# Moving tiles within SBUF: first weights 128 bytes past a multiple of 256, gate tiles 192 past, with no instruction changed

## The chip, the cores and the metric

The kernel runs on one core of one Trainium2 chip. The metric is the device time of one execution in microseconds (us), the median of three runs. TensorE (PE in the profile) multiplies matrices: it loads a stationary operand of 128 x 128 (PEld, LDWEIGHTS) and streams a moving operand past it (PE, MATMUL). Both are read from SBUF; the sums go to PSUM. DVE is VectorE, ACT ScalarE, POOL GpSimd, SP the engine that issues most transfers.

## The reference

Windowed attention with four sink positions over 4 batches, 8 heads, 768 positions and 64 channels, and after it a feed-forward layer over its 3072 rows. Cut to what matters:

```python
scores = scale * np.matmul(q, k.transpose(0, 1, 3, 2))
keep = is_sink | in_window            # n_sink 4, window 128
a = softmax(np.where(keep, scores, -1e9))
x = (a @ v).transpose(0, 2, 1, 3).reshape(3072, 512)
h = x @ w_in                          # 512 x 2048
g = h - np.tanh(h)
out = g @ w_out                       # 2048 x 512
```

Everything is float32.

## The kernel before

The 3072 rows are cut into 12 chunks of 256. Attention for a chunk leaves x transposed in SBUF. The feed-forward layer goes through 8 groups of 256 hidden channels, so there are 12 x 8 = 96 steps of chunk and group, and each step has two halves.

The first half (`mm1`, L700) makes h, 256 hidden channels by 256 rows, as 24 matmuls with a first-weight tile `w0` as the stationary operand (128 x 128) and the chunk's x as the moving one (128 x 256). Float32 accuracy is had from two rounded parts of every operand: `xh` and `xl` are x's high and low part, and a `w0` tile holds a high and a low part too. Each pair of 128 x 128 of weights goes high by `xh`, high by `xl`, low by `xh`.

The gate (`gate`, L705 to L716) is ACT's tanh, DVE's subtraction, ACT's rounding to `gh` and DVE's remainder `gl`. The second half (`mm2`, L748) adds to out 12 matmuls with a slice of `gh` or `gl` as the stationary operand (128 x 128) and a row of the second weights `w1` as the moving one (128 x 512). Step n's second half stands behind step n + 1's first half on TensorE, so the gate has time.

Attention of later chunks is woven between steps: scores `s` (L496, stationary `q`, moving `ks`, 128 x 260), transposes `t` (L575, stationary the probabilities `p`, moving the identity), and x (L629, stationary `v`, moving `pt`). The first 12 units of scores take raw float32 operands that lie for that time in the places of weight tiles (L489, `qk`).

A recording layer (`Work`) notes each piece of work with its engine, an estimated duration and a due time, and sets each engine's order before anything runs. It doesn't know addresses.

Tiles lie in SBUF in the order in which their pools are opened: every pool takes the next free bytes of each partition. Slices of `w0`, `w1`, x, `gh` and `gl` that a matmul reads start at multiples of 512 bytes from the start of their tile, so a tile's place modulo 256 is that of all its operands. The scores are the exception: slices of `ks` start 0, 16, 32 or 48 bytes past a multiple of 256, by head and by half of the chunk. `GAP` is 16, the width in float32 of a tile that nothing reads or writes; it only takes 64 bytes.

Of the kernel before, what the change touches and what calls it, by code (L numbers as in the profile page):

```python
# [9 lines left out]
F32 = mybir.dt.float32  # L10
# [8 lines left out]
P = 128  # L19
# [19 lines left out]
GAP = 16  # L39
# [3 lines left out]
def kernel(  # L43
# [50 lines left out]
    with tc.If(bad == 0) as cmp:  # L94
        _banded(tc, qd, kp, vp, vs, masks, w_in, w_out, ident, pts, early, out)
# [146 lines left out]
def _banded(tc, qd, kp, vp, vs, masks, w_in, w_out, ident, pts, early, out):  # L242
    nc = tc.nc
    et = mybir.EngineType
    with ExitStack() as ctx:

        def pool(name, bufs, **kw):
            return ctx.enter_context(tc.tile_pool(name=name, bufs=bufs, **kw))

        pool("gap", 1).tile([P, GAP], F32, tag="gap", name="gap")  # L250
        w0pool, wmpool, kpool = pool("w0pool", 1), pool("wmpool", 2), pool("kpool", 2)
        w1pool, cpool = pool("w1pool", 1), pool("cpool", 1)
        wpools = w0pool, w1pool
        qpool, vpool, hpool = pool("qpool", 2), pool("vpool", 3), pool("hpool", 1)
        xpool, gpool = pool("xpool", 2), pool("gpool", 2)
        spool, pp, sm = pool("spool", 1), pool("pp", 2), pool("sm", 4)
        ps_s, ps_t, ps_x = pool("ps_s", 1, space=PSUM), pool("ps_t", 1, space=PSUM), pool("ps_x", 1, space=PSUM)
        ps_h, ps_o = pool("ps_h", 2, space=PSUM), pool("ps_o", 1, space=PSUM)
        work = Work()
# [794 lines left out]
```

## Time and profile before

| | before |
|---|---|
| time, median of 3 runs | 686.6 us (686.59 to 687.09) |
| the profiled execution: its time | 687.03 us |
| the profiled execution: span from first to last instruction | 685.2 us |
| TensorE busy, matmuls | 671.9 us, 98% of the span |
| TensorE busy, weight loads | 598.4 us, 87% |
| VectorE busy | 426.9 us, 62% |
| ScalarE busy | 366.8 us, 54% |
| TensorE's granted clock, mean | 0.998 of full speed |

A matmul's recorded duration runs from its first read to its last result, and the next one starts long before that end. So the time that a matmul takes from the engine is the distance between starts, or between ends, and not the duration; trains of equal matmuls in the chain of work or in the timeline show it.

### The profile page before, as it was taken

How to read it: one execution, taken by the hardware profiler on the slowest of the kernel's cores; microseconds unless marked ns; L12 is line 12 of the kernel's file. 1: busy time of each engine (PE TensorE's matmuls, PEld its weight loads, DVE VectorE, ACT ScalarE, POOL GpSimd, SP SyncE). 2: the span in 40 equal slices, each digit the busy share in tenths (PEclk: the TensorE clock that was granted, in tenths of full speed). 3: DMA queues.
4: the chain of work that ended last, by engine and by line, in shares of the span. 5: the costliest groups of instructions: out<-in, count | busy, mean ns of one | idle time of the engine just before them, and what ended most of it. 6: DMA issues, size and time to landing. Idle time of an engine off the chain costs nothing.

```text
span 685.2 us, 12423 instructions
## 1 busy us (share of the span) xinstructions
PE 671.9 (98%) x4604; PEld 598.4 (87%) x4604; DVE 426.9 (62%) x1084; ACT 366.8 (54%) x1001; POOL 52.0 (8%) x201
## 2 busy tenths in 40 slices
PE   7999999999999999999999999999999999999996
PEld 5777899999889989989988998998898898998986
DVE  6889999837845647656655665565554755663221
ACT  5996433347754646456545645555555645644222
POOL 6220010000000010000001000001000000000000
PEclk9999999999999999999999999999999999999999
DMA  6789800012221132012103102122112111100000
GB/s 207 242 251 381 345 1 2 4 64 81 55 81 37 30 106 56 28 34 90 48 28 109 55 28 91 28 54 80 38 34 83 55 28 59 59 1 1 32 1 35
DMA packets 31713, 52.14 MB, mean 76 GB/s; under 512 B 3228, under 2 KB 21020, under 8 KB 31644
## 3 DMA queue, kind: packets, MB, share of 16 engines
q1 hardware_dynamic: 31340, 50.93, 22.9%
q8 instruction: 38, 0.62, 0.4%
q10 hardware_dynamic: 304, 0.33, 0.2%
q14 instruction: 31, 0.25, 0.1%
HBM read 44.96 MB, written 6.29 MB: 75 GB/s over the span
## 4 chain that ended last, share of the span: by engine, by line
PE 87%; ACT 6%; DVE 3%; SPq 1%; issue 1%; DMA 0%; POOL 0%; POOLq 0%; ACTq 0%
PE o L748 38%; PE h L700 36%; PE s L496 5%; PE x L629 5%; PE t L575 2%; ACT p L548 2%; ACT p L522 2%; PE x L623 1%; DVE pt L589 1%; DVE pt L169 1%; DMA qk<-qd 0%; ACT gh L712 0%; ACT ks L453 0%; DVE pt L167 0%; PE x L606 0%
## 5 line engine op out<-in xcount | busy, mean ns | idle before, releaser
L700 PE MATMUL h<-xh,w 128*128 128x256 f32 x1536 | 285.5, 281 | 0.0
L700 PEld LDWEIGHTS h<-xh,w 128*128 128x128 f32 x1536 | 240.7, 188 | 1.7 <-issue 0.2
L700 PE MATMUL h<-xl,w 128*128 128x256 f32 x768 | 215.0, 280 | 0.0
L748 PE MATMUL o<-w,gh 128*128 128x512 f32 x768 | 197.2, 397 | 0.8 <-ACT gh L712 0.5
L748 PEld LDWEIGHTS o<-w,gh 128*128 128x128 f32 x768 | 137.7, 188 | 27.7 <-ACT gh L712 2.1
L700 PEld LDWEIGHTS h<-xl,w 128*128 128x128 f32 x768 | 146.3, 191 | 1.4
L748 PE MATMUL o<-w,gl 128*128 128x512 f32 x384 | 104.9, 394 | 0.0
L705 ACT ACTIVATE graw<-h 128x512 f32<-128x512 f32 x96 | 56.9, 592 | 89.7 <-PE h L700 89.7
L522 ACT ACTIVATE p<-p,st 128x132 f32<-128x132 f32 x192 | 76.1, 399 | 52.3 <-DVE st L514 51.4
L716 DVE TENSOR_TENSOR gl<-h,gh 128x512 fp32r<-128x512 f32 x96 | 66.1, 688 | 48.8 <-ACT gh L712 48.6
L708 DVE TENSOR_TENSOR h<-h,graw 128x512 f32<-128x512 f32 x96 | 66.4, 691 | 44.4 <-ACT graw L705 44.0
L748 PEld LDWEIGHTS o<-w,gl 128*128 128x128 f32 x384 | 70.8, 188 | 15.0 <-issue 1.0
L712 ACT CAST gh<-h 128x512 fp32r<-128x512 f32 x96 | 55.6, 579 | 49.9 <-DVE h L708 49.8
L508 DVE COPY_PREDICATED s<-above,s 128x256 f32<-128x256 uint32 x80 | 34.0, 425 | 72.6 <-PE s L496 72.4
L548 ACT ACTIVATE p<-p,st 128x132 f32<-128x132 f32 x192 | 61.9, 396 | 5.7 <-DVE st L543 5.3
L514 DVE CUSTOM_DVE_ANT_0 p<-s,mask 128x132 f32<-128x132 f32 x192 | 48.9, 292 | 8.6 <-POOL qraw L347 2.7
L553 POOL CAST z<-p 128x16 fp32r<-128x16 f32 x48 | 10.2, 213 | 495.8 <-ACT p L548 493.9
L496 PE MATMUL s<-ks,q 128*128 128x260 f32 x288 | 46.2, 282 | 0.0
L463 ACT CAST q<-qraw 128x512 fp32r<-128x512 f32 x36 | 22.4, 622 | 43.8 <-PE s L496 41.8
L496 PEld LDWEIGHTS s<-ks,q 128*128 128x128 f32 x288 | 42.3, 188 | 4.0 <-issue 0.4
L645 DVE TENSOR_TENSOR xl<-x,xh 128x512 fp32r<-128x512 f32 x24 | 16.5, 688 | 44.3 <-ACT xh L641 44.3
L458 DVE TENSOR_TENSOR ks<-kraw,ks 64x392 fp32r<-64x392 f32 x72 | 40.4, 561 | 2.2
(77 smaller groups left out, 574.2 us busy)
## 6 DMA issues: line engine op xcount, KB each, us to landing
qraw<-qd SPq DMA_DIRECT2D x36, 256.0 KB, 2.7
wraw<-w_in SPq DMA_DIRECT2D x16, 512.0 KB, 8.1
wraw<-w_out SPq DMA_DIRECT2D x16, 512.0 KB, 10.0
kraw<-kp SPq DMA_DIRECT2D x37, 196.0 KB, 2.6
v<-vp SPq DMA_DIRECT2D x27, 256.0 KB, 2.9
out<-ob SPq DMA_DIRECT2D x24, 256.0 KB, 2.2
qk<-kp SPq DMA_DIRECT2D x8, 196.0 KB, 5.0
qk<-qd SPq DMA_DIRECT2D x16, 64.0 KB, 4.7
```

Of the source, the lines that this page charges most:

```text
L458: nc.vector.tensor_tensor(k[o, h, :], t[r, :], k[r, h, :].bitcast(F32), op=ALU.subtract)
L496: nc.tensor.matmul(ps[h][:, :WIN], lhsT=q[:, h, t * P : (t + 1) * P], rhs=rhs, start=i == 0, stop=i == 1,)
L514: nc.vector.tensor_tensor_reduce(out=pr[u][:, j, :], in0=ps[h][:, P:WIN], in1=mask[:, kind, :], scale=-0.125, scalar=BIG, op0=ALU.add, op1 ...
L522: nc.scalar.activation(e, e, AF.Exp, bias=st[u][:, j : j + 1], scale=-1.0, accum_out=st[u][:, 4 + j : 5 + j],)
L548: nc.scalar.activation(pr[u][:, j, :], pr[u][:, j, :], AF.Copy, scale=s[:, 8 + j : 9 + j])
L629: nc.tensor.matmul(xps[key][(p - p0) // 2][h * 64 : h * 64 + 64, p % 2, a:z], lhsT=vt[cc, i][:, hd : hd + D], rhs=rhs, start=False, stop=p ...
L700: nc.tensor.matmul(hps[n][:, f, :], lhsT=w, rhs=x, start=r == 0, stop=r == 11)
L705: nc.scalar.activation(gr[n], hps[n], AF.Tanh)
L708: nc.vector.tensor_tensor(hps[n], hps[n], gr[n], op=ALU.subtract)
L712: nc.scalar.copy(gh[n], hps[n])
L716: nc.vector.tensor_tensor(gl[n], hps[n], gh[n].bitcast(F32), op=ALU.subtract)
L748: nc.tensor.matmul(ops[cc, t], lhsT=(gh, gh, gl)[i][n][:, f, t * P : (t + 1) * P], rhs=wt[1, g][:, (0, 1, 0)[i], f, :], start=first and no ...
```

## The change

The pools are opened in another order, and the filling tile is 128 bytes instead of 64 and stands elsewhere. No instruction is added, removed or moved: on every engine the order of instructions is the same in both programs. Only the places in SBUF differ. In bytes past a multiple of 256:

| tile | read by | before | after |
|---|---|---|---|
| `w0` (first weights), and `qk` lent from them | weight loads of L700 | 64 | 128 |
| `xh`, `xl` | moving operand of L700 | 0 | 0 |
| `gh`, `gl` | weight loads of L748 | 0 | 192 |
| `w1` (second weights) | moving operand of L748 | 0 | 0 |
| `q`, `ks` of later chunks | L496 | 0 | 0 |
| `p` of later chunks (two buffers) | weight loads of L575 | 0, 64 | 128, 192 |
| `p` and `ob` in `wmpool` | L575, stores | 64, 128 | 0, 64 |
| `kraw` (two buffers) | ACT, DVE, first units' L489 | 192, 224 | 0, 32 |
| `graw` | DVE | 0 | 192 |
| `vsink` | weight loads of L623 | 0 | 192 |

Modulo 512 the same holds with `w0` at 320 before and 384 after, and `gh`, `gl` at 0 and 192.

```diff
-        pool("gap", 1).tile([P, GAP], F32, tag="gap", name="gap")
-        w0pool, wmpool, kpool = pool("w0pool", 1), pool("wmpool", 2), pool("kpool", 2)
+        wmpool, w0pool, pp = pool("wmpool", 2), pool("w0pool", 1), pool("pp", 2)
         w1pool, cpool = pool("w1pool", 1), pool("cpool", 1)
         wpools = w0pool, w1pool
         qpool, vpool, hpool = pool("qpool", 2), pool("vpool", 3), pool("hpool", 1)
-        xpool, gpool = pool("xpool", 2), pool("gpool", 2)
-        spool, pp, sm = pool("spool", 1), pool("pp", 2), pool("sm", 4)
+        xpool, kpool = pool("xpool", 2), pool("kpool", 2)
+        pool("gap", 1).tile([P, 2 * GAP], F32, tag="gap", name="gap")
+        gpool, spool, sm = pool("gpool", 2), pool("spool", 1), pool("sm", 4)
```

## Rows read from the trace of the kernel before

**Rows 1.** The page: busy time, share of the span and instructions of each engine, and TensorE's granted clock in 40 slices of the span (9 is 90% or more).

```profile
PE 671.9 (98%) x4604; PEld 598.4 (87%) x4604; DVE 426.9 (62%) x1084; ACT 366.8 (54%) x1001; POOL 52.0 (8%) x201
PEclk9999999999999999999999999999999999999999
```

**Rows 2.** Who waited for whom, TensorE's matmuls: us in total, times, longest.

```profile
PE warm L92 <- POOL pt L105: 3.3, 1, 3.3
PE t L575 <- DVE pt L589: 1.3, 2, 0.9
PE t L575 <- ACT p L548: 0.8, 1, 0.8
...
PE o L748 <- ACT gh L712: 0.5, 2, 0.3
```

**Rows 3.** The page's groups: line, engine, operation, output and operands, shapes, count; busy us, mean ns of one; idle time before.

```profile
L700 PE MATMUL h<-xh,w 128*128 128x256 f32 x1536 | 285.5, 281 | 0.0
L700 PE MATMUL h<-xl,w 128*128 128x256 f32 x768 | 215.0, 280 | 0.0
L748 PE MATMUL o<-w,gh 128*128 128x512 f32 x768 | 197.2, 397 | 0.8 <-ACT gh L712 0.5
L748 PE MATMUL o<-w,gl 128*128 128x512 f32 x384 | 104.9, 394 | 0.0
L496 PE MATMUL s<-ks,q 128*128 128x260 f32 x288 | 46.2, 282 | 0.0
...
L700 PEld LDWEIGHTS h<-xl,w 128*128 128x128 f32 x768 | 146.3, 191 | 1.4
```

**Rows 4.** The chain of work that ended last, its 25 longest pieces in order of time: start us, us, engine, output and line, count of instructions. Of L700 the list has three trains of 48 at 5.45 us, all shown, ten of 48 at 5.65 and five of 42 at 4.95, of which the first and the last stand here.

```profile
273.39 5.47 PE o L748 x24
279.33 5.65 PE h L700 x48
292.57 4.95 PE h L700 x42
308.93 5.45 PE h L700 x48
...
418.24 5.45 PE h L700 x48
...
545.96 5.50 PE o L748 x24
...
581.54 5.45 PE h L700 x48
...
635.33 5.65 PE h L700 x48
...
669.47 4.95 PE h L700 x42
```

**Rows 5.** Groups of matmuls (PE) and of weight loads (PEld) in two stretches inside trains of L700, columns as in rows 3: first 311.5 to 314.2 us, then 323.9 to 326.6 us.

```profile
L700 PE MATMUL h<-xh,w 128*128 128x256 f32 x17 | 3.0, 277 | 0.0
L700 PEld LDWEIGHTS h<-xl,w 128*128 128x128 f32 x8 | 1.5, 188 | 0.0
...
L700 PE MATMUL h<-xh,w 128*128 128x256 f32 x16 | 2.9, 281 | 0.0
L700 PEld LDWEIGHTS h<-xl,w 128*128 128x128 f32 x8 | 1.5, 192 | 0.0
```

**Rows 6.** Two trains of L748 in the timeline, eight matmuls with `gh` and four with `gl` each: start us, us from the first start to the last end, instruction, count. Then their groups, columns as in rows 3, in the stretch of each.

```profile
138.34 2.00 PE L748 MATMUL o<-w,gh 128*128 128x512 f32 x8
140.19 1.07 PE L748 MATMUL o<-w,gl 128*128 128x512 f32 x4
...
548.58 1.98 PE L748 MATMUL o<-w,gh 128*128 128x512 f32 x8
550.39 1.07 PE L748 MATMUL o<-w,gl 128*128 128x512 f32 x4
...
L748 PE MATMUL o<-w,gh 128*128 128x512 f32 x7 | 1.8, 393 | 0.0
...
L748 PE MATMUL o<-w,gh 128*128 128x512 f32 x8 | 2.0, 389 | 0.0
```

**Rows 7.** The chain from 305 to 355 us, short pieces between the trains, columns as in rows 4.

```profile
308.45 0.48 PE s L496 x4
...
314.38 0.44 PE t L575 x4
314.82 2.75 PE o L748 x12
317.57 0.47 PE s L496 x4
...
318.74 2.74 PE o L748 x12
```

**Rows 8.** Engines in three stretches of the steps: us, busy us of each engine and instructions, clock, DMA share, GB/s.

```profile
60.00:158.50 98.50, 98.05 (x638) 88.53 (x637) 83.33 (x107) 40.92 (x68) 2.75 (x3) 1.00 0.29 113
186.00:440.00 254.00, 253.74 (x1812) 228.84 (x1811) 150.43 (x398) 138.08 (x378) 14.31 (x60) 1.00 0.19 57
440.00:684.00 244.00, 239.76 (x1664) 215.64 (x1662) 120.95 (x312) 117.35 (x311) 10.52 (x45) 1.00 0.13 39
```

**Rows 9.** The gate tile `gh`: instructions that write or read it, count, duration in ns (least, median, most), first and last start.

```profile
L712 ACT CAST gh<-h x96: 558/586/598, 55.4 to 675.9; 128x512 fp32r<-128x512 f32 x96
L716 DVE TENSOR_TENSOR gl<-h,gh x96: 676/690/693, 56.9 to 676.5; 128x512 fp32r<-128x512 f32 x96
```

**Rows 10.** The page's groups of small matmuls whose stationary tile moves, and its transfers: tiles, queue, count, KB each, median us from issue to landing.

```profile
L575 PE MATMUL t<-ident,p 128*128 128x128 f32 x192 | 29.4, 275 | 2.5 <-DVE pt L589 1.3 <-ACT p L548 0.8 <-ACT pt L582 0.4
L489 PE MATMUL s<-qk 128*128 128x260 f32 x64 | 16.1, 390 | 0.2 <-DVE st L514 0.2
L623 PE MATMUL x<-zr,vsink 128*128 128x512 f32 x24 | 8.5, 417 | 0.2 <-ACT zr L613 0.2
...
wraw<-w_in SPq DMA_DIRECT2D x16, 512.0 KB, 8.1
wraw<-w_out SPq DMA_DIRECT2D x16, 512.0 KB, 10.0
```

## Prediction

> **What bounds the kernel now.** I read the page's first two parts first. TensorE is busy for 98% of the span at full granted clock, in every slice [rows 1]. Then who waited for whom: all waits of matmuls for other engines come to some 7 us, nearly half of it the start [rows 2]. Then the engines by stretch: in three stretches of 596.5 us together PE's busy time is within 5 us of the time itself, and the next engine, DVE, is busy 85% of the first and 50 to 60% of the others [rows 8]. So the time is TensorE's queue of matmuls, end to end. What a matmul takes there decides, and the change can touch nothing else that counts: it moves no instruction.
>
> The groups give mean durations of 281 ns for L700 and 394 to 397 for L748 [rows 3], but matmuls overlap, so I divide trains by their counts. A train of 48 of L700 takes 5.45 us, or 5.65 [rows 4]. That is **113.5 ns or 117.7 ns a matmul**, and nothing in between: the 42s, at 4.95, are 117.9. The same instructions on the same tiles have both. In the list three trains of 48 run at the lower level and fifteen trains (690 matmuls of 834, 83%) at the upper. Within a lower train a matmul lasts 277 ns, within an upper one 281, and there the weight loads that run beside it last 192 instead of 188 for the `xl` matmuls [rows 5]. So when it is slow, both reads are slow: stream and weight load disturb each other, and a whole train stays in whichever pattern it fell into.
>
> L748 has steps too. Eight with `gh` and four with `gl` that stand right behind a first half take 2.00 and 1.07 us; a train in the middle takes 1.98 and 1.07. Less the last one's duration, that is (2.00 - 0.393) / 7 = 229.6 ns against (1.98 - 0.389) / 7 = 227.3, and (1.07 - 0.389) / 3 = 227.0 in the calm part [rows 6]. Long trains mean 5.47 / 24 = 227.9 to 5.50 / 24 = 229.2 [rows 4], trains of 12 some 228.3 to 229.2 [rows 7]. So the floor is **227 ns**, a disturbed matmul loses about 4 (393 against 389), and the average is 228.8: L748 mostly runs undisturbed already.
>
> Here is what the trace says on places. `gh` by `w1` is at distance 0 and mostly calm; `w0` by x is at distance 64 and mostly disturbed. The scores are at distances 0, 16, 32 and 48, and four take 0.47 to 0.48 us, 118 to 120 ns [rows 7], where 260 columns at the lower level would be 113.5 x 260 / 256 = 115.3. No row has distance 128 or 192.
>
> **The change part by part.** The sum is made against the profiled execution, 687.03 us (its span 685.2 and 1.8 around it), 0.4 us above the median of 686.6; I take differences from it and put them on the median.
>
> *First weights to 128 (L700, 2304 matmuls).* The difference of the levels is 117.7 - 113.5 = 4.2 ns. If all fell to the lower level: 2304 x 0.83 x 4.2 ns = 8.0 us gained. If all rose to the upper: 2304 x 0.17 x 4.2 = 1.6 us lost. If they met twice where they now meet once, another 2304 x 4.2 = 9.7 us lost. I take a reversal of the mixture to some 30% at the upper level: 2304 x 0.53 x 4.2 = **5.1 us gained**. My reason is thin and I say so: the present distance sits on its bad pattern four times in five, so another distance has more room to be better than worse, and a calm pattern, once entered, lasts for a whole train in rows 4.
>
> *Gate tiles to 192 (L748, 1152 matmuls).* All calm: 1152 x 1.8 ns = 2.1 us gained. All disturbed once: 1152 x (231 - 228.8) = 2.5 us lost; twice (235): 7.1 us lost. A 512-column stream lasts twice as long as the weight load beside it, so it has a calm half in which to get back in step, as it does now within a train. I take **nothing**.
>
> *Scores, unmoved (288).* They stand between the others and inherit their pattern: at most 288 x 4.2 = 1.2 us either way. I take nothing.
>
> *Probabilities, `vsink`, raw units.* Transposes follow each other in 0.44 / 4 = 110 ns [rows 7]; there are 192 of them, 24 sums with `vsink` and 64 raw scores on lent places [rows 10]. One step of 4.2 ns on all 280 is 1.2 us, either sign; nothing taken.
>
> *Other engines.* 96 `gl` instructions lie within 676 to 693 ns and 96 `gh` within 558 to 598 [rows 9], and DVE and ACT have room [rows 8]. If the new places of `gh`, `graw` and `kraw` cost DVE or ACT a few per cent, TensorE would cover it: the gate has a whole first and second half, 2.7 to 2.8 us each, and its longest wait on TensorE is now 0.3 us (0.5 us in two) [rows 2].
>
> *Transfers.* The first weights land in 8.1 us at 64 past, the second in 10.0 at multiples [rows 10]: no price of the place is visible, and their lead is covered after the start. Nothing.
>
> Sum: 686.6 - 5.1 = **681.5 us**.
>
> One rule of the Trainium skill speaks against any effect at all. "TensorE: Matmul & The Clock Gate" (section "Step-by-step: what each phase is for") says that TensorE has two independent SBUF read ports, and that loading the next weights takes no read bandwidth from the running matmul. By it the sum would be 686.6, no change. The rows at two levels, with weight loads of 188 and 192 ns that go with them, disagree with it in this kernel; that the distance of the two places is what matters is not shown by any row.
>
> **The rivals.** *The gates leave their calm place.* Distance 0 is the only one with long calm trains of L748, and the change gives it up. If L748 is disturbed once or twice a matmul (+2.5 to +7.1 us) and L700 goes wholly to its upper level (+1.6), the time is 690.7 to 695.3; I take 692. For it: the scores, mostly at distances other than 0, average 2 to 5 ns above their floor. Against it: L700 at 64 can be calm. It decides once L748 averages above about 230 ns with L700 no better. With L700's second meeting, 9.7 more: 702 to 705.
>
> *Nothing changes.* The level is set by the order in which trains follow each other (what stood before, when it ended) and not by the places; then the mixture stays, 686.6 within 1.4 us. For it: one distance shows both levels. Against it: the trains' pattern comes from two reads, and reads have places.
>
> *Lower than the lower level.* The 113.5 could itself hold a meeting that another distance avoids. Transposes with the same 128 x 128 weight load follow each other in 110 ns [rows 7], so L700 could not be shorter than that: 2304 x (0.83 x 7.7 + 0.17 x 3.5) ns = 16.1 us, 670.5. Against it: no train of L700 has it.
> "TensorE: Matmul & The Clock Gate" (section "Back-to-back issue gap") gives columns over 2.4 GHz plus 2.5 ns, an estimate of 109.2 ns for 256 columns and 215.8 for 512, under every train here. By it there would be more to gain than I count.
>
> **How the numbers follow.** Changes under 0.2% (1.4 us) can't be told from none here. Faster as forecast: 0.43, its own range 676 (8.0 + 2.1 + half a microsecond of scores gained) to 685.2. Below the lower level: 0.06. Nothing: 0.17. The gates' rival, with L700's second meeting: 0.34. So faster 0.49, same 0.17, slower 0.34. The range for 8 in 10 goes from 675 to 695: below it stays most of the 0.06, above it the second meeting and the worst of the gates, about 0.12.
>
> **What would show it.** Right: the chain has most trains of 48 of L700 at 5.45 us, the mean of L700's matmuls falls from 281 towards 277 ns and its `xl` weight loads from 191 towards 188 [rows 3, 5], while eight of `gh` stay at 1.98 to 2.00 us. The gates' rival: eight of `gh` over 2.02 us, trains of 24 over 5.55. Nothing: the mixture of 5.45 and 5.65 as now. Below: trains of 48 under 5.4 us. Wrong in another way: waits of TensorE for DVE or ACT above the 7 us of now, or `gl` and `gh` instructions longer than they are, so that a shorter first half is lost to the gate.

## The result and the profile after

The changed kernel takes 691.56 us (691.28 to 691.78) against 686.6: a ratio of 1.0069, with a 95% interval of 1.0058 to 1.0079. It is **slower by 5.0 us** between the medians (4.7 by the ratio, with 4.0 to 5.4 in its interval), where 5.1 us less were forecast. The profiled execution has 691.5 us and a span of 689.7, 4.5 more than before.

The page after, the lines that answer to [rows 1, 3], and under them who waited for whom, as in [rows 2]:

```profile
PE 677.2 (98%) x4604; PEld 603.2 (87%) x4604; DVE 427.8 (62%) x1084; ACT 367.6 (53%) x1001; POOL 52.4 (8%) x201
PEclk9999999999999999999999999999999999999999
L700 PE MATMUL h<-xh,w 128*128 128x256 f32 x1536 | 290.1, 282 | 0.0
L700 PEld LDWEIGHTS h<-xh,w 128*128 128x128 f32 x1536 | 242.5, 188 | 1.7 <-issue 0.2
L700 PE MATMUL h<-xl,w 128*128 128x256 f32 x768 | 216.3, 282 | 0.0
L748 PE MATMUL o<-w,gh 128*128 128x512 f32 x768 | 197.5, 398 | 0.4 <-ACT gh L712 0.3
...
L748 PE MATMUL o<-w,gl 128*128 128x512 f32 x384 | 106.0, 397 | 0.0
...
PE t L575 <- DVE pt L589: 1.3, 2, 0.9
...
PE o L748 <- ACT gh L712: 0.3, 1, 0.3
```

Clock and waits are as before, and DVE and ACT are busy as long as before within 1 us. What grew is TensorE's own busy time, 671.9 to 677.2 us. By groups, L700 goes from 285.5 + 215.0 to 290.1 + 216.3, 5.9 us more, and L748 from 302.1 to 303.5; matmuls of different groups overlap, so these add up to more than the 5.3 us.

The chain after, in order of time, some of its longest pieces as in [rows 4]:

```profile
475.90 5.76 PE h L700 x48
488.64 5.70 PE h L700 x48
501.25 5.71 PE h L700 x48
...
543.76 4.99 PE h L700 x42
549.66 5.52 PE o L748 x24
```

No train of 48 stands at 5.45 or at 5.65 us any more. There are two new levels: 5.70 / 48 = 118.8 ns and 5.76 / 48 = 120.0 ns a matmul; the 42s are 118.8. Both lie above the upper level of before, 117.7. The train of 24 of L748 takes 5.52 us, where before the longest took 5.50. In the slower level of L700 both reads last longer, as in [rows 5]; the groups from 313.3 to 315.9 us, then from 326.1 to 328.5 us:

```profile
L700 PE MATMUL h<-xl,w 128*128 128x256 f32 x8 | 2.3, 285 | 0.0
L700 PEld LDWEIGHTS h<-xh,w 128*128 128x128 f32 x15 | 2.4, 191 | 0.0
...
L700 PE MATMUL h<-xl,w 128*128 128x256 f32 x7 | 2.0, 282 | 0.0
L700 PEld LDWEIGHTS h<-xh,w 128*128 128x128 f32 x14 | 2.1, 188 | 0.0
```

For a measure over a whole run I take the distance between the ends of neighbouring matmuls in the trace and average it over a line, pauses left out. L700 goes from 116.8 to 118.8 ns, and the ends of all 2304 sum to 4.6 us more; L748 from 229.4 to 230.7, and as its first matmuls wait a little less, the sum grows by 0.6 us only; the rest, mostly raw scores and transposes, gives back 0.7. That is the 4.5 us of the span.

### The profile page after: what moved, and what is told of

It reads as the page before. It is cut to its first block, busy times and chain, and to the rows that moved or that the text cites. A ratio compares the mean times of both kernels' runs of the same rounds, so it can differ in the third digit from the quotient of the medians.

```text
span 689.7 us, 12423 instructions
## 1 busy us (share of the span) xinstructions
PE 677.2 (98%) x4604; PEld 603.2 (87%) x4604; DVE 427.8 (62%) x1084; ACT 367.6 (53%) x1001; POOL 52.4 (8%) x201
## 4 chain that ended last, share of the span: by engine, by line
PE 90%; ACT 4%; DVE 3%; SPq 1%; issue 1%; DMA 0%; POOL 0%; POOLq 0%; ACTq 0%
PE h L700 38%; PE o L748 38%; PE s L496 5%; PE x L629 5%; PE t L575 2%; ACT p L548 1%; ACT p L522 1%; PE x L623 1%; DVE pt L589 1%; DVE pt L169 1%; DMA qk<-qd 0%; DVE pt L167 0%; PE x L606 0%; DVE p L514 0%; SPq L106 0%
## 5 line engine op out<-in xcount | busy, mean ns | idle before, releaser
L700 PE MATMUL h<-xh,w 128*128 128x256 f32 x1536 | 290.1, 282 | 0.0
L700 PEld LDWEIGHTS h<-xh,w 128*128 128x128 f32 x1536 | 242.5, 188 | 1.7 <-issue 0.2
L700 PE MATMUL h<-xl,w 128*128 128x256 f32 x768 | 216.3, 282 | 0.0
L748 PE MATMUL o<-w,gh 128*128 128x512 f32 x768 | 197.5, 398 | 0.4 <-ACT gh L712 0.3
L748 PEld LDWEIGHTS o<-w,gh 128*128 128x128 f32 x768 | 137.7, 188 | 27.0 <-ACT gh L712 1.2
L700 PEld LDWEIGHTS h<-xl,w 128*128 128x128 f32 x768 | 144.7, 188 | 1.7
L748 PE MATMUL o<-w,gl 128*128 128x512 f32 x384 | 106.0, 397 | 0.0
L748 PEld LDWEIGHTS o<-w,gl 128*128 128x128 f32 x384 | 70.9, 188 | 15.8 <-issue 1.0
L496 PEld LDWEIGHTS s<-ks,q 128*128 128x128 f32 x288 | 42.7, 188 | 4.1
L496 PE MATMUL s<-ks,q 128*128 128x260 f32 x288 | 46.1, 282 | 0.0
```

What stands on the lines that cost most here:

```text
L496: nc.tensor.matmul(ps[h][:, :WIN], lhsT=q[:, h, t * P : (t + 1) * P], rhs=rhs, start=i == 0, stop=i == 1,)
L700: nc.tensor.matmul(hps[n][:, f, :], lhsT=w, rhs=x, start=r == 0, stop=r == 11)
L748: nc.tensor.matmul(ops[cc, t], lhsT=(gh, gh, gl)[i][n][:, f, t * P : (t + 1) * P], rhs=wt[1, g][:, (0, 1, 0)[i], f, :], start=first and no ...
```

## Experiments

Each is the kernel before the change with another order of pools and other fillings; no instruction differs, and each computes everything. An edit is written as the order of pools in one line, numbers being bytes of filling, "mid" standing for `cpool`, `qpool`, `vpool`, `hpool`, `xpool`. The order before is `64 w0 wm k w1 mid g s pp sm`. Where the edit changes the number of lines, the profile's line numbers shift with it (in the first run below, L698 is L700). "Distance" is the place of the stationary operand less that of the moving one, modulo 256. A train is "calm" where it runs at the lower of the two levels of before, 113.5 ns for L700, and "settled" figures leave out its beginning.

**One part at a time.** In the first run `p`, `ob` and `kraw` stand as in the change too; the third run moves such tiles by themselves.

```diff
-64 w0 wm k w1 mid g s pp sm
+wm w0 pp w1 mid g s k sm            # first weights alone: 128
```

> First weights alone moved to 128 past, gate tiles at 0 as before; p, ob and kraw stand as in the change. Theory distance (each line's spacing is set by the distance of its own two operands modulo 256): L700 goes from 116.8 to 118.8 ns a matmul as in the change (2304 x 2.0 ns = 4.6 us), L748 stays at 229.4: 691.2 us, no train of 48 of L700 at 5.45 us. Theory handoff (what stood before a train decides its pattern, so the gates' place decides how L700 begins): L700 stays near 116.8 ns, 687 us. Theory others (p, ob, kraw or vsink cost it): 691 us with L700 as in the change only if p, ob or kraw is the cause, which the run that moves these alone tells apart.

Measured: 693.36 us, ratio 1.0090 (1.0073 to 1.0107). L700 119.8 ns, its sum 6.9 us over before; L748's sum 0.1 us under. The first weights alone cost more than the whole change: 6.5 us between the medians. Its chain:

```profile
476.60 5.76 PE h L698 x48
489.30 5.76 PE h L698 x48
...
569.84 5.04 PE h L698 x42
605.63 5.49 PE o L746 x24
```

Every train of 48 is at the new slowest level, 120 ns, while L748's 24 are as before.

```diff
-64 w0 wm k w1 mid g s pp sm
+k w0 wm 64 w1 mid pp 64 g s sm      # gate tiles alone: 192
```

> Gate tiles (and graw, vsink) alone moved to 192 past, first weights at 64 as before. Theory distance: L700 stays at 116.8 ns with both levels, L748 goes from 229.4 to 230.7 ns (1152 x 1.3 ns = 1.5 us): 687 to 688 us. Theory handoff: L700 goes to 118.8 ns although its own operands stand as before, 691 to 692 us.

Measured: 685.23 us, ratio 0.9980 (0.9970 to 0.9989): faster, by 1.6 us between the medians. The ten times go from 684.35 to 686.9, and the trace is that of the fastest, so its gains are at the upper end. In it L748 rises to 230.1 ns, 0.4 us in sum. L700, whose operands have not moved, falls to 115.8 ns, 2.5 us in sum. The theory of handoff had the right line and the wrong sign. Its chain:

```profile
106.61 2.73 PE h L700 x24
...
471.35 5.65 PE h L700 x48
...
484.11 5.47 PE h L700 x48
...
598.74 5.50 PE o L748 x24
604.72 5.46 PE h L700 x48
```

The levels of L700 are those of before, 113.5 to 114 and 117.7, but ten of the fifteen trains of 48 now fall into the lower.

So the change is the sum of a loss and a gain: 6.9 - 2.5 = 4.4 us of L700's time, against 4.6 measured in the change itself. The medians say the same with a smaller gain: 6.5 - 1.6 = 4.9 us, against 5.0.

```diff
-64 w0 wm k w1 mid g s pp sm
+k w0 pp 64 w1 mid g wm s sm         # the other tiles alone
```

> First weights at 64 and gate tiles at 0 as before; kraw at 0 and 32, ob and p of wmpool at 0 and 64, p of later chunks at 64 and 128, vsink at 128. Theories distance and handoff: 686.6 us, L700 116.8 and L748 229.4 ns, within 0.7 us. Theory others: up to 691 us.

Measured: 687.12 us, ratio 1.0002 (0.9992 to 1.0012). L700 116.9 ns, L748 229.8. The tiles of `p`, `ob`, `kraw` and `vsink` cost nothing that can be told here, though not each of them stands exactly where the change puts it.

```diff
-64 w0 wm k w1 mid g s pp sm
+pp 64 w0 wm k w1 mid g s sm         # all by 128 further
```

> First weights, x, gate tiles, second weights, q and ks all 128 bytes further than before: first weights 192, all the others 128 past, so every distance is as before. Theory distance: 686.6 us, trains of 48 of L700 at 5.45 and 5.65 us as before. Rival, absolute places (an operand that doesn't start at a multiple of 256 is read more slowly by itself): all streams now start 128 past, so L700 and L748 both slower, 690 us or more.

Measured: 686.69 us, ratio 0.9992 (0.9982 to 1.0002). L700 116.8, L748 229.3. A shift by 128 that all these operands share costs nothing: what counts is where they stand to each other.

**Other distances.** In the four that follow one tile stands elsewhere and the rest as before.

```diff
+w0 w1 mid g s wm k pp sm            # first weights at 0
+k wm w0 64 w1 mid g s pp sm         # first weights at 192
+64 w0 wm k w1 mid pp g s sm         # gate tiles at 128
+64 w0 wm k w1 mid 64 g s pp sm      # gate tiles at 64
```

> First weights at distance 0 from x, gate tiles at 0 from w1. Theory ladder (L700 gets slower the further its two operands are apart modulo 256, 64 being 116.8 ns and 128 119.8): under 116.8 ns, 684 us or less. Theory overtaking (the stream reads twice as fast as the weight load and passes it every 256 bytes; at distance 0 it does so at the start, in the middle and at the end of a weight load, elsewhere twice): above 119.8 ns, 694 us or more. L748 stays at 229.4 to 230.2 in both.

Measured: 691.88 us, ratio 1.0073 (1.0044 to 1.0102). All long trains of L700 are alike, 5.75 / 48 = 119.8 ns. The ladder falls: 64 is better than both its neighbours. The theory of overtaking had the right direction but asked for more, 694 us.

> First weights at distance 192 (64 the other way round), gate tiles at 0. Theory mirror (only how far apart modulo 256, in either direction): as at 64, 116.8 ns for L700, 687 us. Theory ladder by distance ahead (0, 64, 128, 192 slower and slower): above 119.8 ns, 694 us or more. Theory that 128 is the one bad place: 117 ns or less.

Measured: 687.75 us, ratio 1.0017 (1.0005 to 1.0028). L700 117.7 ns, fifteen of fifteen trains of 48 at 5.65 or 5.66 us. So 192 has the upper level of 64 but not the lower one, which only one train of 18 and two of 6 show; the mirror holds for half.

> First weights at 64, gate tiles at 128. Theory distance alone: L748 leaves 229.4 for 230 to 234 ns (0.7 to 5.3 us), L700 stays at 116.8. Theory handoff beside it: L700 changes too, towards 115.8 as with the gates at 192 (2.4 us gained) or to its upper level everywhere, 117.8 (2.3 us lost).

Measured: 685.81 us, ratio 0.9983 (0.9972 to 0.9994). L748 232.6 ns, 3.7 us lost; L700 114.9 ns, 4.3 us gained. Its chain shows both, trains of L748 at 5.58 / 24 = 232.5 ns and L700 mostly calm:

```profile
497.31 5.46 PE h L700 x48
...
599.61 5.58 PE o L748 x24
605.67 5.46 PE h L700 x48
```

> First weights at 64, gate tiles at 64, so both lines are at one distance. Theory that a pattern goes on unbroken when both lines stand at the same distance: a train of L700 that begins calm stays calm, L700 below 115.8 ns, 683 to 685 us. Theory distance alone: L700 116.8, L748 230 or more, 687 us or more.

Measured: 688.33 us, ratio 1.0025 (1.0014 to 1.0037). L748 233.1 ns, 4.3 us lost; L700 115.5, 3.2 gained. Half of each expectation came true: L700 is calmer, but L748 pays more than that.

**The handoff alone.** Where L700 follows L748 directly, its first weights are loaded while the last matmul of L748 still streams second weights (in the trace before, all 36 times). Here gate tiles and second weights move together, so that L748 keeps its distance 0 and L700 its 64, and only the first pair changes wherever L748 meets another line (L700, scores or transposes).

```diff
+64 w0 w1 wm k mid 64 g s pp sm      # both at 64
+64 w0 k w1 wm mid pp g s sm         # both at 128
+64 w0 wm w1 k mid pp 64 g s sm      # both at 192
+64 w0 32 w1 wm 32 mid k 32 g s pp sm  # both at 96
```

> First weights at 64 and x at 0 as before; gate tiles and second weights both at 64, so L700 keeps its distance of 64 and L748 its distance of 0. What changes is the first pair of a train: while the last matmul of L748 streams second weights at 64, first weights at 64 are loaded (distance 0; before 64), and while the last of L700 streams x at 0, gates at 64 are loaded (distance 64; before 0). Theory handoff: L748 falls back to 227 ns within a train as before, and L700 begins in another pattern; if that is the calm one everywhere, L700 goes from 116.8 to 113.5 ns (2304 x 3.3 = 7.7 us), 679 us; if the upper one everywhere, 689 us. Theory distance alone: 686.7 us, L700 116.8.

Measured: 685.9 us, ratio 0.9983 (0.9972 to 0.9995). L700 stays at 116.9 ns, so the handoff did not do to it what was expected; the microsecond comes from L748, 228.5.

> As the run with the pair at 64, but gate tiles and second weights both at 128: the first pair of a train of L700 has distance 192, that of L748 128. Theory handoff: L748 at 227 to 230 ns, L700 anywhere from 113.5 (679 us) to 117.8 (689 us), another mixture than before. Theory distance alone: 686.7 us.

Measured: **682.98 us, ratio 0.9943 (0.9921 to 0.9966)**, the fastest of all and faster than both kernels. L700 115.5 ns and 3.2 us less, L748 228.6 and 0.8 us less. Its chain has L700 mostly calm from 278 to 620 us, mostly at the upper level before and after, and trains of L748 as in [rows 4]:

```profile
107.14 2.83 PE h L700 x24
...
326.42 5.49 PE o L748 x24
331.92 0.48 PE s L496 x4
332.40 5.46 PE h L700 x48
...
561.73 4.78 PE h L700 x42
...
631.22 5.65 PE h L700 x48
```

The same places in the chain before:

```profile
102.24 2.83 PE h L700 x24
...
327.82 5.48 PE o L748 x24
333.30 0.48 PE s L496 x4
333.78 5.65 PE h L700 x48
```

So the gain does not come where L700 follows L748 directly: the thirteen trains of 24 that stand between trains of 12 of L748 settle at 117.8 in both. It comes mostly from trains that begin behind four scores, whose own operands didn't move. In each of the two kernels what ran before a train fixes its level: behind 24 of L748 and four scores all six trains of 48 are upper before and calm here, and behind six of L700, 12 of L748 and four scores all ten of 42 likewise; behind a long row of L629, four of L748 and four scores all five of 48 are calm in both. Nor is the first pair all there is: the run with gate tiles at 192 leaves the first pair of L700 as it was, and there those thirteen trains of 24 settle at 113.3.

> As the run with the pair at 64, but gate tiles and second weights both at 192: the first pair of a train of L700 has distance 128, that of L748 192. Theory handoff: L700 anywhere from 113.5 (679 us) to 117.8 (689 us), another mixture than before. Theory distance alone: 686.7 us.

Measured: 686.69 us, ratio 0.9997 (0.9986 to 1.0009). L700 117.2 ns, only one train of 48 at the lower level, L748 229.2: nothing gained.

> First weights at 64, gate tiles and second weights both at 96: a train of L700 begins with a pair at distance 224. Theory handoff: L748 228.5 to 229.5 as with the other pairs, L700 between 113.5 and 117.8 with yet another mixture, 680 to 688 us. Rival, that the pair's place acts in cells of 64 bytes: as with the pair at 64, 116.9 ns, 685.9 us.

Measured: 684.82 us, ratio 0.9969 (0.9958 to 0.9980). L700 115.9 ns, L748 229.7, a little above what was expected of it. Not what the pair at 64 does (116.9), so the place doesn't act in cells of 64 bytes.

**Is there a calm pattern at 128?** The change's distance with the best handoff:

```diff
+wm w0 w1 pp mid k 64 g s sm         # first weights, gates, second weights at 128
```

> First weights at 128 from x as in the change, gate tiles and second weights both at 128, the pair that brought most calm trains when the first weights stood at 64; a train of L700 now begins with a pair at distance 0, one of L748 with 128. Theory that L700 has no calm pattern at 128, whatever a train begins with: no train at 113.5 ns, L700 118.7 to 120 on average (4.3 to 7.3 us over before), 690 to 694 us. Rival, that at 128 it is only not led into its calm pattern by the handoffs tried: trains of 48 at 5.45 us appear, L700 below 118 ns, 688 us or less.

Measured: 692.88 us, ratio 1.0089 (1.0060 to 1.0118). L700 119.7 ns, and not one calm train:

```profile
476.29 5.76 PE h L700 x48
489.05 5.76 PE h L700 x48
...
605.36 5.47 PE o L748 x24
611.32 5.76 PE h L700 x48
```

With this, the first weights alone and the change itself, three arrangements of what runs before have been tried at 128, and no six matmuls in a row averaged under 116.5 ns in any. Distance 128 has no calm pattern that these trains find with any of the three.

**Between the multiples of 64.**

```diff
+32 w0 wm k 32 w1 mid g s pp sm      # first weights at 32
+k 32 w0 wm 32 w1 mid g s pp sm      # first weights at 96
```

> First weights at 32, gate tiles at 0. Distances tried so far settle at 120 ns (0), 113.5 or 117.8 (64), 117.5 to 119 (96), 118.7 to 120 (128), 117.8 (192). Theory of cells of 64 bytes: as 0, 120 ns, 692 us. Theory of a sliding distance: between 0 and 64, 117 to 119.5 ns with no calm train, 687 to 692 us.

Measured: 689.57 us, ratio 1.0042 (1.0022 to 1.0061). L700 118.2 ns, long trains at 5.67 or 5.68 us.

> First weights at 96, between 64 and 128, all else as before. Theory of cells of 64 bytes (all starts within 64 bytes act alike): as 64, L700 116.8 ns, 686.7 us. Theory of a sliding distance: between 116.8 (64) and 119.8 (128), 687 to 693 us.

Measured: 688.67 us, ratio 1.0026 (1.0015 to 1.0038). L700 117.7 ns, long trains at 5.63 to 5.70 us. Both means lie between those of their neighbours: the distance slides.

## Why the prediction was wrong

**The bound was right.** TensorE's queue set the time, no other engine took part, and the difference is found in the spacing of its matmuls: 4.6 us in L700, 0.6 in L748, 0.7 given back by others.

**The step that failed is the first term, first weights to 128: 5.1 us gained, measured 6.9 us lost.** The argument was that 64 sits on its bad pattern four times in five and that another distance has more room to be better. But 64 is the only distance of the six tried (0, 32, 64, 96, 128, 192) at which L700 has the calm pattern in more than 30 of its 2304 matmuls, and its upper level is about as good as the best of the others. The share of bad trains was read as a fault of the distance, where it was a matter of what runs before a train; the distance was the good one. [rows 4, 7] could have warned: that a distance shows a calm pattern at all was the rarer thing, and the scores, at other distances, took 118 to 120 ns.

**The levels are no steps.** The bounds counted a second meeting at another 4.2 ns, 9.7 us in all. The levels at 128 are 120.0 and 118.8 ns, 2.3 or 1.1 above the upper one. So the mean of all upper (1.6 us lost) was too small a bound and the second meeting too large.

**The second term, gates to 192: nothing taken; it gained about 1.5 us by itself.** L748 lost 0.4 us, inside the bounds given. But the reason, a calm half in which the long stream gets back in step, is not borne out: with gate tiles at 64 or 128 L748 averages 233.1 and 232.6 ns. And what was left out is that the operands of L748 change the pattern of L700: up to 2.5 us gained there. Without it the change would have been slower still. The working treated lines one by one, and its rival on trains that follow each other only asked whether nothing would change. (Its average for L748, 228.8 ns, is 229.4 over the whole run, which moves none of its bounds for L748 by more than 0.7 us.)

**The terms of nothing held**: probabilities, `vsink` and `kraw` by the run that moves such tiles alone; scores, which take 119.5 ns before and 119.6 after; the gate's engines and the transfers, in that TensorE waits no longer than before.

**The rivals.** The one that ended on the other side gave 692 us and the measurement is 691.6, but that is luck, for its mechanism is not what happened: L748 was to lose 2.5 to 7.1 us and L700 at most 1.6, and measured were 0.6 and 4.6. One of its signs came even so (L748 averages 230.7, above 230), another not (trains of 24 reach 5.52 us, not 5.55). The sign it gave for L748's own distance is right (0 is the best of four: mostly 227 ns settled, against 229 at 192, 232.5 at 128 and 233 at 64), its size at 192 far too large. "Nothing changes" fell with the run of first weights alone; but half of it is right, for in the kernel before all long trains with the same three stretches ahead of them have the same level. "Lower than the lower level" was never seen: no kernel has a train of 48 under 5.45 us.

The page rule quoted in the prediction, from the Trainium skill's "TensorE: Matmul & The Clock Gate" (section "Step-by-step: what each phase is for"), that a weight load takes no read bandwidth from the running matmul, would by the prediction's reading have made all these kernels alike. They run from 682.98 to 693.36 us with the same instructions in the same order, so the trace disagrees here, for operands of four bytes. The other figure there, 109.2 ns for 256 columns and 215.8 for 512, the Trainium skill's "TensorE: Matmul & The Clock Gate" (section "Back-to-back issue gap") gives for a matmul by itself and not for a stream of pairs of weight load and matmul; the calm levels here are 113.5 and 227 ns.

What stays open is the mechanism below the distances: no record shows which bytes the two reads ask for when, and why 64 has a calm pattern and 128 none is not explained. That 256 bytes are the period is shown for L748 alone. Modulo 512 its operands are 0 apart before and 256 in the four runs that move only the pair, and in most trains of all five it settles at 226.5 to 228 ns. L700 was never run at a distance and at that distance plus 256: modulo 512 its runs stand at 0, 288, 320, 352, 384 and 448, so its period could be longer.

## What to carry to other kernels

Where a kernel is bound by matmuls that each load new weights, divide long trains in the chain by their counts and look for several levels; if there are, the places of the two operands in SBUF modulo 256 bytes are worth a sweep, line by line and with the trains in their real order. Here a level that was sometimes reached showed a good distance that was badly entered: try to change how trains begin (here by moving the operands of the lines before, as a pair) before giving up the distance.

## What the runs showed of the hardware

- For 256 columns of 4-byte operands against a fresh 128 x 128 weight load, trains settle at 120 ns a matmul at distance 0, 118.2 at 32, 113.5 or 117.7 at 64, 117.3 to 118.8 at 96, 118.8 or 120.0 at 128, 117.7 at 192. For 512 columns: mostly 227 ns at 0, 233 at 64, 232.5 at 128, 229 at 192 with some trains at 233.
- Moving the operands of both lines by the same 128 bytes changes neither line's spacing by more than 0.1 ns.
- What runs before a train shows in the whole train. At distance 64 the share of calm trains depends on the places of operands of the lines that ran before, through four scores whose operands did not move, and the average of L700 goes from 114.9 to 117.2 ns with nothing of its own changed.
- 32 bytes are enough to make a difference, at 32 and 96 and in the pair at 96.
